# Retention, expert layers and a Mish layer on one core: one PSUM layout for both parts, a product issued earlier, and a table of weight tasks

## Chip, cores and metric

The kernel runs on 1 core of one Trainium2 chip. The metric is the device time of one execution in microseconds (us). A core has engines with instruction queues of their own: PE (matmuls, with weight loads PEld), DVE, ACT, POOL, and SP, which here issues every DMA.

## What is computed

All data is fp32; N = 1152 tokens, model width 512.

```python
# retention: q, k, v of shape (2, 8, 576, 64)
scores = q @ k^T / 8;  ret = scores * gamma_h ** (row - col) for row >= col, else 0
x = (ret @ v), heads side by side, as (1152, 512)
# four experts, w1 (4, 512, 1024), w2 (4, 1024, 512), p = probs / (sum + 1e-9)
x = sum_e p[:, e] * (relu(x @ w1[e]) @ w2[e])
# one layer, w_in (512, 2048), w_out (2048, 512)
out = (h * tanh(softplus(h))) @ w_out,  h = x @ w_in      # Mish
```

## The kernel before, in words

**Order.** The instruction order on every engine is the order of the program text (`manual_schedule`), so each engine works through its list and stands still at an instruction whose inputs are late.

**Retention** (`retention`, until about 57 us): 8 units of two heads. For unit u PE does `scores(u)`, then `values(u-1)` and `cross(u-1)`, then `state(u)`. DVE multiplies the scores by the decay into `ret` (L292, three instructions, here called the eviction of the scores); ACT and DVE read the state into `sbd`; `cross` splits its output into a rounded part (ACT, L191) and the remainder (L192) in `xop` and `xc`. All three kinds of PSUM tile come from one pool `psum` of four two-bank tiles, in rotation. From unit 3 on, each unit also does one weight task, whose remainder goes to DVE.

**Precision.** Each operand is a sum of a rounded part and a remainder, so a product takes three matmuls (L533, L587, L600, L615).

**Feed-forward** (`feed_forward`): 12 units of 512 hidden columns; units 0 to 7 are the experts (NE = 8), 8 to 11 the Mish layer. A list `seq`, made by `steps()`, gives the order of steps:

- `("S", u, c)`, `first_pair`: the first matrix for two thirds of the tokens, as seven products of Strassen's kind (`PRODUCTS`; operands B11, B21, B22 and the differences T1 to T4 in `xop`), 42 matmuls into four banks. Products 1, 5 and 7 are copied out by ACT to p1, p5, p7 (L545); POOL adds p7 and p1 to p5 (L563, L564); DVE adds these to the other banks (L549); then `hidden` makes the activation on ACT (L514, or Mish at L510 and a copy at L511) and its remainder on DVE (L515, L512).
- `("L", u, c)`, `first_last`: the same matrix for the last third, 24 matmuls into a two-bank tile of the pool `pairs` (two such tiles).
- `("Y", u, c, tb)`, `m2`: the second matrix, also into a tile of `pairs`; DVE adds it into `acc` (L662, L663; L671 and L673 in the Mish layer).

After the last expert, `new_x` makes the Mish layer's input from `acc`: differences on DVE (L640), then `split_x`. The steps there run Y(7,0,2), S(8,0), Y(7,1,2), S(8,1), L(8,0), L(8,1). Index i_x is that of Y(7,0,0) in `seq`; S(8,0) is i_x + 5.

**Weight tasks.** A list `tasks` of 96 entries is worked through in order by `weight_task`: either `weight_sums` (four sums on POOL, L134 to L137, which make a "G" matrix out of an "O" matrix) or `split_w` (ACT rounds, L153; POOL makes the remainder in four instructions, L156). A call that finds its task not yet allowed does nothing. Calls stand after steps, and inside `first_pair` in the list `later`, which is emptied behind product 7. The Mish layer's weights come as float64 and are converted by `turn64` (ACT L463 to L466; DVE L451 to L477) through DRAM.

**Pools.** SBUF and PSUM of the retention part are given back at its end; the pools `banks` (four single banks), `pairs`, `hp`, `accp` and `ph` of the feed-forward part take that space.

The functions as the profile numbers their lines:

Of the kernel before, what the change touches and what calls it, by code (L numbers as in the profile page):

```python
# [78 lines left out]
def retention_moe_mish(ctx: ExitStack, tc: tile.TileContext, q2, k2, kt_in, v, vt_in, probs, w1, w2, w64, cdec, dec, out):  # L79
# [86 lines left out]
    def weight_task(i, lo_engine, only_g=False):  # L166
        if n_task[0] >= len(tasks):
            return
        sums, (m, u, c) = tasks[n_task[0]]
        raw = "O" if m == "G" else m, u, c  # L170
        if raw not in raw_t or not (sums or splits((m, u, c), i) and sums_at.get((m, u, c), -99) <= i - (1 if u == 1 else 2)):
# [24 lines left out]

    with ExitStack() as actx:  # L200
        cst = actx.enter_context(tc.tile_pool(name="cst", bufs=1))
        ld = actx.enter_context(tc.tile_pool(name="ld", bufs=2))
        psum = actx.enter_context(tc.tile_pool(name="psum", bufs=4, space=bass.MemoryType.PSUM))

        def ps_tile():
            return psum.tile([P, 2, 512], F32, tag="ps", name="ps")

        units = [(b, pr) for pr in range(NPAIR) for b in range(B)]
# [73 lines left out]
        def scores(u):  # L282
            qr, kb, pr = q_t[u][0], k_t[u % 2], units[u][1]
            a = ps_tile()
            ret = ld.tile([P, 2, 8 * D], F32, tag="ret", name="ret")
            for c, (w, t, off) in enumerate(BLOCKS):
                pe.matmul(  # L287
                    a[:, t, off:off + w], kb[:, c].rearrange("p j d -> p (j d)"),
                    qr[:, c * D:c * D + w], start=True, stop=True,
                )  # L290
            for t, off, n, w, m in EVAC:
                dve.tensor_tensor(  # L292
                    out=ret[:, t, off:off + n * w].rearrange("p (c n) -> p c n", n=w),
                    in0=a[:, t, off:off + n * w].rearrange("p (c n) -> p c n", n=w),
                    in1=cst_sb[:, pr, m:m + w].unsqueeze(1).to_broadcast([P, n, w]), op=ALU.mult,
                )
            ret_t[u] = ret

        def state(u):
            st = ps_tile()  # L300
            vt, kt = q_t[u][1:3]
            sbd, pr = sbd_t[u % 2], units[u][1]
            for c in range(NCH - 1):
                pe.matmul(
                    st[:, 0, c * P:(c + 1) * P], kt[:, c], vt[:, c].rearrange("p j d -> p (j d)"),
                    start=True, stop=True,
                )
            for c in range(NCH - 1):
                for o in own:
                    src = st[o, 0, c * P + o.start:c * P + o.stop]  # L310
# [41 lines left out]
        def retention():  # L352
# [13 lines left out]
            for j in range(2):  # L366
                dve.memset(v_t[1][own[1 - j], :, j], 0.0)


            warm = [ps_tile() for _ in range(4)]  # L370
            for i in range(4):
                pe.matmul(warm[i][:, 0, :256], zero[:, :P], zero, start=True, stop=True)
            prep(0)
# [5 lines left out]
            for u in range(NUN):  # L379
# [11 lines left out]
                if u >= 3:  # L391
                    weight_task(u - NUN - 2, dve)
                if u == 2:
# [11 lines left out]
                if u == 5:  # L405
                    split_x(xop[:, :, T1], t1, dve)
            cross(NUN - 1, values(NUN - 1))
            dve.tensor_tensor(out=t3, in0=t2, in1=t3, op=ALU.subtract)
# [13 lines left out]
    acc_t = acc.rearrange("p k n -> p (k n)").rearrange("p (t d) -> p t d", d=DM)  # L422
    banks = ctx.enter_context(tc.tile_pool(name="banks", bufs=1, space=bass.MemoryType.PSUM))
    pairs = ctx.enter_context(tc.tile_pool(name="pairs", bufs=2, space=bass.MemoryType.PSUM))

    def ps_tile():
        return pairs.tile([P, 2, 512], F32, tag="ps", name="ps")

# [90 lines left out]
    def first_pair(u, c, early, later, order):  # L519


        o = [
            [banks.tile([P, 512], F32, tag=f"b{t}{j}", name=f"b{t}{j}")[:, :TB] for j in range(2)]
            for t in range(2)
        ]
        h = [h_tile(u, c, i) for i in range(2)]

        def product(n):
            m, kh, fb, r, t, j, opens = PRODUCTS[n]
            w = w_t[m, u, c]  # L530
            for kk in range(2):
                for i, (a, b) in enumerate(((0, 1), (0, 0), (1, 0))):
                    pe.matmul(  # L533
                        o[t][j], w[:, a, 2 * kh + kk, fb * P:(fb + 1) * P], xop[:, b, r, kk],
                        start=opens and kk == 0 and i == 0, stop=kk == 1 and i == 2,
                        skip_group_check=not opens,
                    )
            return o[t][j]

        def tile(name):  # L540
            return ph.tile([P, TB], F32, tag=name, name=name, bufs=1)

        def copy(name, src):
            t = tile(name)
            act.activation(out=t, in_=src, func=AF.Copy)  # L545
            return t

        def add(out, a, b):
            dve.tensor_tensor(out=out, in0=a, in1=b, op=ALU.add)  # L549

        done = {}
        for n in order:
            done[n] = product(n)
            if n == 1:
                p1 = copy("p1", done[n])
            elif n == 5:
                p5 = copy("p5", done[n])
                while early:
                    early.pop(0)()
            elif n == 7:  # L560
                p7 = copy("p7", done[n])

                pool.tensor_tensor(out=p5, in0=p5, in1=p7, op=ALU.add)  # L563
                pool.tensor_tensor(out=p5, in0=p5, in1=p1, op=ALU.add)  # L564
                while later:
                    later.pop(0)()
            elif n == 6:
                p16 = tile("p16")
# [37 lines left out]
    def second_t(u, tts):  # L606

        o = ps_tile()
        for n, tt in enumerate(tts):
            ts = slice(tt % 3 * P, (tt % 3 + 1) * P)  # L610
            for f in range(4):
                h, w = h_t[u, f // 2, tt // 3], w_t["W", u, f // 2]
                w = w.rearrange("p a k c -> p a (k c)")
                for i, (a, c) in enumerate(((0, 1), (0, 0), (1, 0))):
                    pe.matmul(  # L615
                        o[:, n], h[:, c, f % 2, ts], w[:, a, f % 2 * 512:(f % 2 + 1) * 512],
                        start=f == 0 and i == 0, stop=f == 3 and i == 2,
                    )
        return o[:, :len(tts)]
# [12 lines left out]
    def new_x(c, tb, a):  # L632
# [10 lines left out]
        if tb == 2:  # L643
            split_x(xc[:, :, 2 * c:2 * c + 2], a, pool)
        elif (c, tb) != (0, 1):
# [31 lines left out]
    def feed_forward():  # L677
# [117 lines left out]
```

## Time and profile before

| | us |
|---|---|
| median of 3 runs (lowest, highest) | 669.52 (666.72, 670.23) |
| profiled execution: its time | 665.34 |
| profiled execution: span, first to last instruction | 663.3 |
| PE busy in the span | 631.9 |
| POOL, DVE, ACT busy in the span | 376.2, 393.0, 309.8 |

The span is what the trace covers; the profiled execution's own time has 2.0 us more around it. Idle time of an engine costs something only where the chain that ends last runs through it.

### The profile page before, as it was taken

The page shows a single profiled execution, that of the slowest core. Times are in us where ns is not written, and L with a number is a line of the kernel's source. Part 1 is how long each engine was busy: PE and PEld are TensorE (multiplying, and loading weights), DVE is VectorE, ACT ScalarE, POOL GpSimd, SP SyncE. Part 2 cuts the span into 40 slices and gives each one's busy share as a digit, 9 for nine tenths or more (in the row PEclk, how much of TensorE's full clock was granted, in tenths as well). Part 3 has the DMA queues.
Part 4 walks back from the last instruction along what each step waited for, and adds up shares of the span by engine and source line. Part 5 has one row for each costly group of instructions (what it writes and reads, how often), then busy time and mean ns, then how long its engine had stood idle before and what let it go on. Part 6 is the DMA issues. An engine that isn't in the chain of part 4 may idle for free.

```text
span 663.3 us, 9398 instructions
## 1 busy us (share of the span) xinstructions
PE 631.9 (95%) x3560; PEld 609.9 (92%) x3560; DVE 393.0 (59%) x593; ACT 309.8 (47%) x503; POOL 376.2 (57%) x471
## 2 busy tenths in 40 slices
PE   8997999999999999999999999968999979998997
PEld 7997999999999999999999999958998768997986
DVE  4776556567665856667776757474356636626322
ACT  4555463625454534635354543225655834745300
POOL 5691877546747638547737728615676465383200
PEclk9999999999999999999999999988999998998999
DMA  8764313243512414422423504200114323130012
GB/s 293 266 239 131 96 62 98 60 132 93 155 61 79 142 51 138 123 92 70 154 65 120 171 0 155 68 0 33 65 32 128 96 95 127 46 113 32 33 48 95
DMA packets 25622, 67.23 MB, mean 101 GB/s; under 512 B 2978, under 2 KB 7146, under 8 KB 25578
## 3 DMA queue, kind: packets, MB, share of 16 engines
q1 hardware_dynamic: 25578, 66.64, 31.1%
q8 instruction: 28, 0.46, 0.3%
q14 instruction: 16, 0.13, 0.1%
HBM read 55.86 MB, written 10.77 MB: 100 GB/s over the span
## 4 chain that ended last, share of the span: by engine, by line
PE 72%; POOL 10%; DVE 6%; issue 5%; ACT 5%; DMA 2%; SPq 1%; POOLq 0%; DVEq 0%
PE ps L600 28%; PE b L533 20%; PE ps L587 13%; PE ps L615 9%; POOL w L156 5%; PE ps L287 1%; ACT w L153 1%; ACT h L511 1%; PE ps L323 1%; ACT b L510 1%; DMA w<-w 1%; POOL wr L135 1%; DVE x L192 1%; DVE b L549 1%; DMA vr<-v 1%
## 5 line engine op out<-in xcount | busy, mean ns | idle before, releaser
L156 POOL TENSOR_TENSOR w<-wr,w 128x256 fp32r<-128x256 f32 x276 | 213.9, 809 | 183.1 <-ACT w L153 183.1
L600 PE MATMUL ps<-h,w 128*128 128x384 f32 x1152 | 203.6, 334 | 0.2 <-DVE h L515 0.2
L600 PEld LDWEIGHTS ps<-h,w 128*128 128x128 f32 x1152 | 200.0, 188 | 0.5 <-DVE h L515 0.5
L533 PE MATMUL b<-x,w 128*128 128x384 f32 x1008 | 181.2, 337 | 11.3 <-ACT p L545 9.0
L533 PEld LDWEIGHTS b<-x,w 128*128 128x128 f32 x1008 | 176.9, 190 | 12.6 <-issue 11.7
L587 PE MATMUL ps<-xc,w 128*128 128x384 f32 x576 | 107.6, 343 | 9.0 <-DVE acc L673 7.4
L587 PEld LDWEIGHTS ps<-xc,w 128*128 128x128 f32 x576 | 103.7, 194 | 10.4 <-DVE acc L673 8.3
L615 PE MATMUL ps<-w,h 128*128 128x512 f32 x432 | 100.2, 390 | 1.3 <-DVE h L512 1.3
L153 ACT ACTIVATE w<-wr 128x1024 fp32r<-128x1024 f32 x72 | 74.4, 1053 | 51.3 <-POOL wr L137 33.8
L615 PEld LDWEIGHTS ps<-w,h 128*128 128x128 f32 x432 | 80.9, 188 | 18.2 <-DVE h L512 1.7
L662 DVE TENSOR_TENSOR ps<-ps,pb 128x768 f32<-128x768 f32 x42 | 40.4, 962 | 34.1 <-PE ps L600 34.1
L545 ACT ACTIVATE p<-b 128x384 f32<-128x384 f32 x72 | 33.7, 490 | 55.8 <-PE b L533 52.5
L515 DVE SCALAR_TENSOR_TENSOR h<-b,h 128x384 fp32r<-128x384 f32 x64 | 34.4, 555 | 39.2 <-ACT h L514 37.8
L514 ACT ACTIVATE h<-b 128x384 fp32r<-128x384 f32 x64 | 30.9, 489 | 41.4 <-DVE b L549 35.6
L549 DVE TENSOR_TENSOR b<-b,p 128x384 f32<-128x384 f32 x72 | 38.8, 559 | 16.4 <-POOL p L564 16.4
L514 ACT ACTIVATE h<-ps 128x768 fp32r<-128x768 f32 x16 | 13.0, 814 | 60.1 <-PE ps L587 60.1
L663 DVE TENSOR_TENSOR acc<-acc,ps 128x768 f32<-128x768 f32 x42 | 40.1, 954 | 1.4
L512 DVE TENSOR_TENSOR h<-b,h 128x384 fp32r<-128x384 f32 x32 | 17.8, 557 | 33.2 <-ACT h L511 33.2
L563 POOL TENSOR_TENSOR p<-p,p 128x384 f32<-128x384 f32 x24 | 24.6, 1024 | 21.7 <-ACT p L545 21.7
L549 DVE TENSOR_TENSOR p<-b,p 128x384 f32<-128x384 f32 x24 | 13.4, 556 | 31.7 <-PE b L533 24.6
L510 ACT ACTIVATE b<-b 128x384 f32<-128x384 f32 x32 | 15.3, 477 | 34.0 <-DVE b L549 28.1
L477 DVE TENSOR_TENSOR g<-g,e 128x512 f32<-128x512 f32 x32 | 30.2, 942 | 1.1
(78 smaller groups left out, 600.4 us busy)
## 6 DMA issues: line engine op xcount, KB each, us to landing
wr<-w SPq DMA_DIRECT2D x32, 512.0 KB, 4.1
w<-w SPq DMA_DIRECT2D x32, 512.0 KB, 4.2
O<-g SPq DMA_DIRECT2D x16, 256.0 KB, 4.3
W<-g SPq DMA_DIRECT2D x16, 256.0 KB, 4.3
wr<-O SPq DMA_DIRECT2D x8, 512.0 KB, 3.3
wr<-W SPq DMA_DIRECT2D x8, 512.0 KB, 3.3
vr<-v SPq DMA_DIRECT2D x8, 288.0 KB, 5.8
pb<-p_dram SPq DMA_DIRECT2D x12, 192.0 KB, 4.8
```

The source lines that it names most:

```text
L153: act.activation(out=w[:, 0], in_=t, func=AF.Copy)
L156: lo_engine.tensor_tensor(out=w[:, 1, k], in0=t[:, k], in1=f32(w[:, 0, k]), op=ALU.subtract)
L514: act.activation(out=out[:, 0], in_=src, func=AF.Relu)
L515: dve.scalar_tensor_tensor(out=out[:, 1], in0=src, scalar=0.0, in1=f32(out[:, 0]), op0=ALU.max, op1=ALU.subtract)
L533: pe.matmul(o[t][j], w[:, a, 2 * kh + kk, fb * P:(fb + 1) * P], xop[:, b, r, kk], start=opens and kk == 0 and i == 0, stop=kk == 1 and i == 2,
L545: act.activation(out=t, in_=src, func=AF.Copy)
L549: dve.tensor_tensor(out=out, in0=a, in1=b, op=ALU.add)
L587: pe.matmul(o[:, j], w[:, a, k, j * P:(j + 1) * P], xc[:, b, k], start=k == 0 and n == 0, stop=k == 3 and n == 2,)
L600: pe.matmul(o[:, j, :TB], w[:, a, 2 * i + f, ds_], h[:, c, f], start=i == f == n == 0, stop=i == f == 1 and n == 2,)
L615: pe.matmul(o[:, n], h[:, c, f % 2, ts], w[:, a, f % 2 * 512:(f % 2 + 1) * 512], start=f == 0 and i == 0, stop=f == 3 and i == 2,)
L662: dve.tensor_tensor(out=o, in0=o, in1=pbb, op=ALU.mult)
L663: dve.tensor_tensor(out=a, in0=a, in1=o, op=ALU.add)
```

## The change

- The pools `banks` and `pairs` are opened ahead of retention and serve both parts. Scores use the two banks `b01` and `b11` (one buffer), the state `b00` and `b10` in turn, values the two tiles of `pairs`.
- Product 1 of S(0,0) and its copy p1 are issued ahead of `values` and `cross` of the last retention unit. p1 and p5 move to a pool `sums` that is open from the start.
- The weight tasks of retention units 6 and 7 put the remainder on POOL.
- In `new_x`, both subtractions for T2 and T4 come one after the other, and the splits of T2, T4 and `xc` are put into `early`, which `first_pair` empties behind product 5's copy.
- `second_t` loops over the halves of the hidden columns outside and the token tiles inside.
- From i_x on, two tables, `n_later` and `n_end`, say how many weight tasks follow product 7 and each step; a split may come one step after its sums.

```diff
-... sums_at.get((m, u, c), -99) <= i - (1 if u == 1 else 2)):
+... sums_at.get((m, u, c), -99) <= i - (1 if u == 1 or u > NE else 2)):
...
+    banks = ... "banks", bufs=1, PSUM;  pairs = ... "pairs", bufs=2, PSUM;  sums = ... "sums", bufs=1
+    def bank(t, j):
+        return banks.tile([P, 512], F32, tag=f"b{t}{j}", name=f"b{t}{j}")
...
-        psum = actx.enter_context(tc.tile_pool(name="psum", bufs=4, ...PSUM))
...
-            a = ps_tile()                      # scores
+            a = [bank(t, 1) for t in range(2)]
...
-            st = ps_tile()                     # state
+            st = bank(u % 2, 0)
...
-                    weight_task(u - NUN - 2, dve)
+                    weight_task(u - NUN - 2, dve if u < 6 else pool)
...
+            o[0][0] = bank(0, 0)[:, :TB]
+            p = product(0, 0, 1, o)
+            ahead_of[0, 0] = o[0][0], p, copy_sum("p1", sums, p)
             cross(NUN - 1, values(NUN - 1))
...
         for n in order:                        # first_pair
-            done[n] = product(n)
+            done[n] = pre[1] if pre and n == 1 else product(u, c, n, o)
             if n == 1:
-                p1 = copy("p1", done[n])
+                p1 = pre[2] if pre else copy_sum("p1", sums, done[n])
...
-        for n, tt in enumerate(tts):           # second_t
-            for f in range(4):
+        for k in range(2):
+            for n, tt in enumerate(tts):
+                for f in range(2):
...
         if tb == 2:                            # new_x
-            split_x(xc[:, :, 2 * c:2 * c + 2], a, pool)
+            early.append(lambda: split_x(xc[:, :, 2 * c:2 * c + 2], a, pool))
...
-            difference(T2, b22, b11)
-            difference(T4, b21, b11)
+            dve.tensor_tensor(out=b11, in0=b22, in1=b11, op=ALU.subtract)
+            dve.tensor_tensor(out=b21, in0=b21, in1=b11, op=ALU.subtract)
+            early.append(lambda: (split_x(xop[:, :, T2], b11, dve), split_x(xop[:, :, T4], b21, dve)))
...
+        n_later = {5: 2, 7: 1, 12: 1, 16: 1, 20: 2, 26: 1, 30: 2, 36: 1}
+        n_end = {0: 1, 8: 2, 10: 2, 14: 2, 17: 1, 18: 1, 21: 1, 23: 2, 27: 1, 28: 1, 31: 1, 33: 1, 34: 1}
...
-                later.extend([lambda: weight_task(i, pool)] * (2 if u in (0, NE) else 1))
+                later.extend([lambda: weight_task(i, pool)] * (n_later.get(i - i_x, 0) if i > i_x else 2 if u == 0 else 1))
...
-            if i_x <= i < i_x + 9:
-                n = (1, 1, 0, 0, 0, 0, 0, 0, 2)[i - i_x]
+            if i >= i_x:
+                n = n_end.get(i - i_x, 0)
...
-                n = 2 if (m, c) == ("L", 0) or u == 0 or u >= NE else 1
+                n = 2 if (m, c) == ("L", 0) or u == 0 else 1
```

## Rows read from the trace of the kernel before

**Rows 1.** Waits of PE, whole span: who waited, for whom; total us, times, longest.

```profile
PE b L533 <- ACT p L545: 9.0, 2, 8.9
PE ps L587 <- DVE acc L673: 7.4, 2, 4.2
PE b L533 <- DVE xc L192: 2.2, 1, 2.2
PE ps L587 <- DVE acc L671: 1.6, 1, 1.6
...
PE ps L615 <- DVE h L512: 1.3, 1, 1.3
```

**Rows 2.** Windows: length; busy us (count) of PE, PEld, DVE, ACT, POOL; granted clock; DMA.

```profile
57.20:59.40 2.20, 0.00 (x1) 0.04 (x1) 1.07 (x3) 1.03 (x3) 0.00 (x0) 1.00 0.41 93
...
86.00:418.00 332.00, 332.00 (x1917) 332.00 (x1917) 222.70 (x311) 155.61 (x241) 208.12 (x256) 1.00 0.33 103
...
441.20:450.00 8.80, 0.01 (x1) 0.00 (x0) 5.58 (x7) 2.98 (x5) 0.37 (x1) 0.64 0.00 0
450.00:452.00 2.00, 1.93 (x6) 1.96 (x7) 0.00 (x0) 1.59 (x2) 1.45 (x1) 0.50 0.00 0
```

**Rows 3.** Chain that ended last: start, us, what; stretches on PE behind its waits.

```profile
547.88 6.74 PE ps L587 x24
...
601.20 5.77 PE ps L587 x24
606.97 8.20 PE ps L615 x36
```

**Rows 4.** Timeline, end of retention: start, us, engine, line, op, count [idle before, releaser].

```profile
46.25 2.22 PE L287 MATMUL ps<-qr,k 128*128 128x128 f32 x18
46.53 1.29 DVE L292 TENSOR_TENSOR ret<-ps,cst_sb 128x384 f32<-128x384 f32 x3
...
51.48 1.23 DVE L156 TENSOR_TENSOR w<-wr,w 128x1024 fp32r<-128x1024 f32 x1 [1.16 <-ACT w L153]
...
53.44 2.29 PE L323 MATMUL ps<-ret,v 128*128 128x128 f32 x18 [1.36 <-DVE ret L292]
...
59.40 2.34 PE L533 MATMUL b<-x,w 128*128 128x384 f32 x12 [2.24 <-DVE xc L192]
...
65.54 0.84 ACT L545 ACTIVATE p<-b 128x384 f32<-128x384 f32 x2
66.06 5.48 PE L533 MATMUL b<-x,w 128*128 128x384 f32 x30 [0.16 <-ACT p L545]
```

**Rows 5.** Timeline between the experts and the Mish layer, step S(8,0).

```profile
441.14 0.94 DVE L640 TENSOR_TENSOR acc<-acc 128x768 f32<-128x768 f32 x1
...
445.85 0.96 DVE L192 TENSOR_TENSOR x<-acc,x 128x768 fp32r<-128x768 f32 x1 [0.91 <-ACT x L191]
...
447.72 0.95 DVE L663 TENSOR_TENSOR acc<-acc,ps 128x768 f32<-128x768 f32 x1
...
449.46 0.85 ACT L545 ACTIVATE p<-b 128x384 f32<-128x384 f32 x2
...
450.07 7.25 PE L533 MATMUL b<-x,w 128*128 128x384 f32 x30 [8.87 <-ACT p L545]
450.33 1.28 ACT L510 ACT_TABLE_LOAD   x1
```

**Rows 6.** Timeline in the Mish layer, steps S(9,1) and S(10,0) and what follows.

```profile
514.23 1.06 ACT L153 ACTIVATE w<-wr 128x1024 fp32r<-128x1024 f32 x1 [3.88 <-POOL wr L137]
...
527.62 8.78 POOL L156 TENSOR_TENSOR w<-wr,w 128x256 fp32r<-128x256 f32 x12 [8.56 <-ACT w L153]
...
539.62 1.01 POOL L563 TENSOR_TENSOR p<-p,p 128x384 f32<-128x384 f32 x1
...
546.61 1.21 DVE L673 TENSOR_TENSOR acc<-acc,ps 128x1024 f32<-128x1024 f32 x1
```

More of the change, by code (lines that the diff above doesn't have):

```diff
@@ L170, in weight_task @@
         raw = "O" if m == "G" else m, u, c
-        if raw not in raw_t or not (sums or splits((m, u, c), i) and sums_at.get((m, u, c), -99) <= i - (1 if u == 1 else 2)):
+        if raw not in raw_t or not (sums or splits((m, u, c), i) and sums_at.get((m, u, c), -99) <= i - (1 if u == 1 or u > NE else 2)):
             return
@@ L194, in retention_moe_mish, with ps_tile, product, sum_tile @@
     ctx.enter_context(tc.manual_schedule())
+    banks = ctx.enter_context(tc.tile_pool(name="banks", bufs=1, space=bass.MemoryType.PSUM))
+    pairs = ctx.enter_context(tc.tile_pool(name="pairs", bufs=2, space=bass.MemoryType.PSUM))
+    sums = ctx.enter_context(tc.tile_pool(name="sums", bufs=1))
+    def bank(t, j):
+        return banks.tile([P, 512], F32, tag=f"b{t}{j}", name=f"b{t}{j}")
+    def ps_tile():
+        return pairs.tile([P, 2, 512], F32, tag="ps", name="ps")
+    def product(u, c, n, o):
+        m, kh, fb, r, t, j, opens = PRODUCTS[n]
+        w = w_t[m, u, c]
+        for kk in range(2):
+            for i, (a, b) in enumerate(((0, 1), (0, 0), (1, 0))):
+                pe.matmul(
+                    o[t][j], w[:, a, 2 * kh + kk, fb * P:(fb + 1) * P], xop[:, b, r, kk],
+                    start=opens and kk == 0 and i == 0, stop=kk == 1 and i == 2,
+                    skip_group_check=not opens,
+                )
+        return o[t][j]
+    def sum_tile(name, of):
+        return of.tile([P, TB], F32, tag=name, name=name, bufs=1)
+    def copy_sum(name, of, src):
+        t = sum_tile(name, of)
+        act.activation(out=t, in_=src, func=AF.Copy)
+        return t
+    ahead_of = {}
     with ExitStack() as actx:
@@ L367, in retention @@
                 dve.memset(v_t[1][own[1 - j], :, j], 0.0)
-            warm = [ps_tile() for _ in range(4)]
             for i in range(4):
-                pe.matmul(warm[i][:, 0, :256], zero[:, :P], zero, start=True, stop=True)
+                pe.matmul(ps_tile()[:, 0, :256], zero[:, :P], zero, start=True, stop=True)
             prep(0)
@@ L406, in retention @@
                     split_x(xop[:, :, T1], t1, dve)
+            o = [[None] * 2 for _ in range(2)]
+            o[0][0] = bank(0, 0)[:, :TB]
+            p = product(0, 0, 1, o)
+            ahead_of[0, 0] = o[0][0], p, copy_sum("p1", sums, p)
             cross(NUN - 1, values(NUN - 1))
@@ L519, in first_pair @@
     def first_pair(u, c, early, later, order):
[L522 to L525, printed above, removed]
+        pre = ahead_of.pop((u, c), None)
+        o = [[pre[0] if pre and t == j == 0 else bank(t, j)[:, :TB] for j in range(2)] for t in range(2)]
         h = [h_tile(u, c, i) for i in range(2)]
[L528 to L546, printed above, removed]
         def add(out, a, b):
@@ L552, in first_pair @@
         for n in order:
-            done[n] = product(n)
+            done[n] = pre[1] if pre and n == 1 else product(u, c, n, o)
             if n == 1:
-                p1 = copy("p1", done[n])
+                p1 = pre[2] if pre else copy_sum("p1", sums, done[n])
             elif n == 5:
-                p5 = copy("p5", done[n])
+                p5 = copy_sum("p5", sums, done[n])
                 while early:
@@ L560, in first_pair @@
             elif n == 7:
-                p7 = copy("p7", done[n])
+                p7 = copy_sum("p7", ph, done[n])
                 pool.tensor_tensor(out=p5, in0=p5, in1=p7, op=ALU.add)
@@ L567, in first_pair @@
             elif n == 6:
-                p16 = tile("p16")
+                p16 = sum_tile("p16", ph)
                 add(p16, done[n], p1)
@@ L608, in second_t @@
         o = ps_tile()
-        for n, tt in enumerate(tts):
-            ts = slice(tt % 3 * P, (tt % 3 + 1) * P)
-            for f in range(4):
[L612 to L618, printed above, removed]
+        for k in range(2):
+            w = w_t["W", u, k].rearrange("p a k c -> p a (k c)")
+            for n, tt in enumerate(tts):
+                h, ts = h_t[u, k, tt // 3], slice(tt % 3 * P, (tt % 3 + 1) * P)
+                for f in range(2):
+                    for i, (a, c) in enumerate(((0, 1), (0, 0), (1, 0))):
+                        pe.matmul(
+                            o[:, n], h[:, c, f, ts], w[:, a, f * 512:(f + 1) * 512],
+                            start=k == f == i == 0, stop=k == f == 1 and i == 2,
+                        )
         return o[:, :len(tts)]
```

15 lines of the change are left out of this document (4 added, 11 removed).

## The prediction

> **What bounds the kernel now.** I read first the windows, to see where PE is full; then the list of PE's waits; then the chain that ended last, for what PE does behind each wait; and last the timeline at each wait, for the reason.
>
> From 86 to 418 us PE is busy without a pause at the full clock: 1917 matmuls in 332 us, 0.173 us each [rows 2]. So a product (6 matmuls) takes 1.04 us, an S step 7.3 us, an L step 4.16 us. In this stretch nothing can be won but by less PE work, and the change removes no matmul. What can be won lies in PE's waits [rows 1], which stand in three places:
>
> - the hand-over from retention to the experts: 2.2 us;
> - S(8,0), the first step of the Mish layer: 8.9 us;
> - the Mish layer: 7.4 us in two waits on L673 (4.2 and so 3.2), 1.6 us on L671 and 1.3 us on L512.
>
> Behind the long ones PE also runs slower. While it stood 8.8 us the granted clock was 0.64 on the mean, and in the next 2 us it was 0.50, the lower level of 1.2 GHz [rows 2]. The 30 matmuls there took 7.25 us; at the full pace they would take 5.2 and the last one's drain of 0.15, so 1.9 us was lost to the clock [rows 5]. The 24 matmuls behind the two L673 waits took 6.74 and 5.77 us in place of 4.16 [rows 3]: 2.6 and 1.6 us lost. All together the waits and the clock hold 21.4 + 6.1 = 27.5 us. That is nearly all that the change can win.
>
> **Part A: retention, PSUM and the early product.** The scores now have one slot, so scores(u+1) cannot start before the eviction of scores(u) has left the first bank. Where is that late? For unit 7: PE issued scores(7) at 46.25, but the eviction of scores(6) began only at 46.53, and its first two of three instructions end near 47.4 [rows 4]. So scores(7) starts about 1.15 us later. Against that, DVE loses the 1.23 us remainder that stood ahead of the eviction of scores(7), and with it the wait of 1.36 us at values(7) [rows 4]. PE's list after 47.4 is scores(7), values(6), cross(6), state(7), some 5.7 us by the starts of before (53.44 less the wait of 1.36, less 46.25, is 5.83), then product 1 (1.04 us): values(7) starts near 54.2 in place of 53.44. cross(7) still ends near 57.15 (59.40 less 2.24), because its last pieces wait for the state's way through ACT and DVE, which the later start does not touch: that chain covers the 0.8 us, and if it did not, they would be paid. The remainder of that weight task on POOL, four pieces of 0.73 us [rows 6], delays the sums queued behind it to about 58 us; those are needed by a split that ACT reaches only at about 63.4 (65.54 less two roundings of 1.06 [rows 4, 6]).
>
> From 57.15 on, product 5 runs at once (its bank is no longer held by the old pool), then the first L step (24 matmuls, issued by `early`) waits for the last `xc` remainder at 59.3, as the products did before. It ends at 63.5, product 2 at 64.5. Product 3 must wait for the copy p5. ACT reaches the p copies at 65.54 behind the splits of T3, T2, T4 and two weight tasks, all unchanged; p5 is now the first of them and ends at 66.0. Before, five products were left at 66.06; now four are left at 66.05. Gain: 1.0 us. Bounds: 0 (the late scores are not covered) to 2.4 us (no wait is left).
>
> **Part B: S(8,0).** Before, ACT's copies p1 and p5 stood at 449.46 behind four splits that each waited on DVE, and product 2 stood behind p1 [rows 5]. Now they stand behind the split of T3 alone, so they are done when products 1 and 5 are (441.2 and 0.5 us more), and products 2, 3 and 7 follow without a wait, to 444.3. DVE: the T2 subtraction starts at 441.14 as before, T4's follows (0.97 each), then the multiply and add of Y(7,0,2) (0.95 each) to 445.0, then the remainders of T2 and T4 (0.96 each) to 446.0 and 446.9. Product 6 waits for T2: 1.7 us. ACT: roundings of T2 and T4 as soon as their subtractions end, then the rounding of `xc`, which needs the add at 445.0, to 445.9; then the table load of 1.28 us, the Mish and its copy, taken at half a microsecond each like a p copy, to 448.2; then p7, to 448.6. Product 4 adds to p7's bank and so waits 1.6 us; it ends at 449.7. Before, the step's 30 matmuls ended at 457.15. Gain: 7.4 us. What is late next is p7, behind the table load. Bounds: 5.5 us (the clock falls again and takes the same 1.9) to 10.8 (8.9 and 1.9: nothing waits). The two waits left are each shorter than the 2.2 us at 57.20, through which the clock stayed at 1.00 [rows 2]; I take 7.4.
>
> The Trainium skill speaks against that: in TensorE: Matmul & The Clock Gate, section HAM oscillation, it says that pauses between bursts of matmuls send the engine back to the slow clock and that this returns pause after pause. By it the sum would be 1.9 us smaller here; the trace has shorter pauses that did not do it and longer ones that did.
>
> **Part C: the Mish layer.** Before, up to two weight tasks followed every step, as early as allowed, so they bunched. At 527.62 twelve remainder pieces ran on POOL for 8.78 us, then four sums to 539.6, and only then L563, the addition to p5 that S(10,0)'s last activations need [rows 6]. The evacuation at 546.61 stands behind these on DVE; PE's next L step wants that tile of `pairs`. Counted through `seq` with both rules, all 96 tasks still get a turn. Behind S(10,0) the tasks of steps i_x+18 and i_x+19 were two W splits, an O split and the sums; now one W split stands there, and the other W and the O split come behind product 7, after POOL's additions. The same holds for S(11,0) ten steps on. So at both places POOL is free when p7 comes, the evacuation moves ahead by some 7 us, more than the wait: 7.4 + 2.6 + 1.6 = 11.6 us.
>
> The 1.6 us at L671 follow from S(9,1), where ACT stood 3.88 us for the sums ahead of a split [rows 6]; those sums now come behind the additions, and the split a step later: 1.55. The 1.3 us on L512 come mostly from the float64 conversions on ACT ahead of the L step's Mish, which stay; only the sums on POOL ahead go. Half: 0.65, with bounds 0 and 1.3. Sum: 13.8 us.
>
> What the later splits cost: W of (9,1) and (10,1) now ends after its Y step begins, some 2.3 us into it. `second_t`'s new order needs it only from half of the first 24 matmuls on, 2.7 us (0.228 each from 36 in 8.20) [rows 3]; I count nothing, with 0.4 us to spare. The split of G(10,0) ends just as product 5 of S(10,0) asks for it. If that cover fails, PE waits up to one split there and in S(11,0): 2 times four pieces of 0.73, 5.8 us, and the clock may fall after each (2.1 on the mean of the two L673 cases): 4.2 more. So the lower bound of C is 3.8, the upper 14.5. SP's queue carries the loads in the same order; each now stands behind a later split, but 4 to 6 steps before its use.
>
> **Sum.** 1.0 + 7.4 + 13.8 = 22.2 us. The profiled execution took 665.34 (span 663.3 and 2.0 around it), so 643.1. The runs' median is 669.52, 4.2 us above it; in the same ratio I forecast 647 us.
>
> **Rivals.**
> 1. *The late splits come too late* (the cover above fails at both places): 22.2 - 10.0 = 12.2 us of gain, 653.1, or 657 on the scale of the median. For it: no margin at G(10,0). Against it: POOL has idle time ahead of each. 0.14.
> 2. *The clock falls in the waits left* in S(8,0) and at the hand-over, 1.9 us each: 18.4 us of gain, 651. For it: two pauses follow each other closely in both places. Against it: the wait at 57.20. 0.12. The page of the Trainium skill named under part B states this rule.
> 3. *PE's waits only move*: the evacuations stay behind the float64 work on DVE and ACT, and the tiles of `pairs` are as late as now; then part C gives about nothing, A and B are lost to new waits for POOL. No change, 669. Against it: the waits follow POOL's additions in the timeline. 0.03.
> 4. *Slower: the table starves the steps.* Each of S(9,1), S(10,0), S(10,1), S(11,0), S(11,1) waits for its G: sums 3.2, rounding 1.06, remainder 2.9 [rows 6], 7.2 us, 36 in all, so 14 us slower, 683. It decides from 4.5 us a place. Against it: the sums come one to three steps (4 to 16 us) ahead of the split, and that again as far ahead of the use. 0.03.
>
> **Chances and range.** The forecast, with part A between its bounds, holds 0.68 (644 to 651). A measurement of this kernel can tell about 0.5% (3.3 us) from no change. Faster: 0.68 + 0.14 + 0.12 = 0.94; same 0.03; slower 0.03. The range goes from 639 (28 us, all waits gone, from the lowest run 666.7) to 657 (rival 1).
>
> **What would show it.** Right: no wait of PE above 2 us behind 60 us; the clock at 1.00 from 441 to the end; POOL's L563 within 1 us of p7 in S(10,0) and S(11,0); scores(7) waiting on L292. In S(8,0) two waits, on T2's remainder (L192) and on p7. Wrong: PE waiting for L156 inside an S or Y step of the Mish layer (rival 1), 0.50 behind S(8,0) (rival 2), or L673 still releasing L587 (rival 3).

## The result and the profile after

The changed kernel takes 649.74 us (median of 4 runs, 647.24 to 652.29) against 669.25 for the kernel before beside it: ratio 0.9714, 95% interval 0.966 to 0.9768. The profiled execution took 647.88 with a span of 645.9, so 17.4 us lie between the two profiles, where the sum said 22.2.

The lines have new numbers in the changed kernel: products L214 (L533 before), L steps L593 (L587), Y steps L606 and L621 (L600, L615), scores L318 and their eviction L323 (L287, L292), p copies L226 (L545), POOL's addition to p5 L569 (L563), Mish remainder L540 (L512), and the evacuation, DVE's add of a Y step into `acc`, L681 (L673). Kernels below shift some of them by a few lines.

First the waits of PE over the whole span of the changed kernel, to be held against [rows 1] (who waited, for whom; total us, times, longest). The wait of 8.9 us on the copies is gone; the two that stand under that name now are one of 2.7 at the hand-over and one of 1.4 in S(8,0). The wait for the evacuation is down from 7.4 to 1.7, but not gone.

```profile
PE b L214 <- ACT p L226: 4.0, 2, 2.7
...
PE b L318 <- DVE ret L323: 2.7, 2, 2.0
...
PE ps L593 <- DVE acc L681: 1.7, 2, 1.3
PE b L214 <- DVE x L192: 1.6, 1, 1.6
...
PE ps L621 <- DVE h L540: 0.6, 1, 0.6
```

Where the 17.4 us come from, by the start of the same step on PE in both traces:

| from, to | before, us | after, us | won | forecast |
|---|---|---|---|---|
| start to S(0,1) | 75.54 | 74.87 | 0.67 | 1.0 (A) |
| S(8,0) to S(8,1) | 22.36 | 17.63 | 4.73 | 7.4 (B) |
| S(9,0) to the last 108 matmuls | 149.48 | 137.63 | 11.85 | 13.8 (C) |

The starts, before and then after (timeline of PE; S(8,0) and S(8,1) of the changed kernel stand under part B; the last group of a window is cut at its end):

```profile
75.54 6.75 PE L533 MATMUL b<-x,w 128*128 128x384 f32 x38
438.96 2.25 PE L533 MATMUL b<-x,w 128*128 128x384 f32 x12
461.32 7.54 PE L533 MATMUL b<-x,w 128*128 128x384 f32 x42
485.22 5.04 PE L533 MATMUL b<-x,w 128*128 128x384 f32 x28
634.70 5.64 PE L615 MATMUL ps<-w,h 128*128 128x512 f32 x24
```

```profile
74.87 7.44 PE L214 MATMUL b<-x,w 128*128 128x384 f32 x42
479.74 7.47 PE L214 MATMUL b<-x,w 128*128 128x384 f32 x42
617.37 22.87 PE L621 MATMUL ps<-w,h 128*128 128x512 f32 x100
```

The three sum to 17.25; the rest is 0.1 us at L(8,0) and the tail. In the profiles each part won, and each won less than forecast.

**Part A in the trace.** The timeline of PE at the end of retention, to be held against [rows 4] (start, us, what, count [idle before, releaser]):

```profile
47.70 2.29 PE L318 MATMUL b<-qr,k 128*128 128x128 f32 x18 [1.99 <-DVE ret L323]
...
57.24 1.34 PE L214 MATMUL b<-x,w 128*128 128x384 f32 x6
58.42 4.32 PE L593 MATMUL ps<-xc,w 128*128 128x384 f32 x24
62.58 1.20 PE L214 MATMUL b<-x,w 128*128 128x384 f32 x6
66.44 4.43 PE L214 MATMUL b<-x,w 128*128 128x384 f32 x24 [2.65 <-ACT p L226]
```

scores(7) waits 1.99 us for the eviction of scores(6). Product 5 follows cross(7) at once, and the first L step starts behind it at 58.42 without the expected wait for the last `xc` remainder; so all the idle time gathers ahead of product 3, 2.65 us where 1.6 was forecast. The order on the engines is the forecast one, the sizes are not. And of the 0.67 us, 0.59 were there at scores(1), the first step that could wait for the one scores slot: it starts at 12.20 here and at 12.79 before, a start that moves from profile to profile (12.20 to 14.21 with the new layout, 12.60 to 13.01 with the old). Counted from scores(1), part A gave 0.08 us.

Why no more? The p copies, on which product 3 waits, stand on ACT behind its read of the last piece of cross(7). The lines are before's read, then the changed kernel's, and the `xc` remainder that the L step was to wait for:

```profile
57.19 0.33 ACT L347 ACTIVATE xf<-ps 128x192 f32<-128x192 f32 x1 [2.00 <-PE ps L333]
```

```profile
57.57 0.33 ACT L378 ACTIVATE xf<-ps 128x192 f32<-128x192 f32 x1 [1.76 <-PE ps L364]
...
59.07 0.56 DVE L192 TENSOR_TENSOR xc<-ps,xc 128x384 fp32r<-128x384 f32 x1 [0.56 <-ACT xc L191]
```

From this read to the products behind the p copies it is 8.87 us in both kernels (66.06 before, 66.44 now). Counted from scores(1), the read comes at 44.40 before and at 45.37 now, 0.97 us later, and that takes back nearly all of the 1.04 us of the product issued early.

**Part B in the trace.** The timeline of PE, to be held against [rows 5], and the windows over the same stretch (columns as in [rows 2]):

```profile
438.31 5.39 PE L214 MATMUL b<-x,w 128*128 128x384 f32 x30
445.28 1.33 PE L214 MATMUL b<-x,w 128*128 128x384 f32 x6 [1.58 <-DVE x L192]
447.98 2.29 PE L214 MATMUL b<-x,w 128*128 128x384 f32 x6 [1.37 <-ACT p L226]
450.06 6.04 PE L606 MATMUL ps<-h,w 128*128 128x384 f32 x24
455.94 7.44 PE L214 MATMUL b<-x,w 128*128 128x384 f32 x42
```

```profile
446.60:448.00 1.40, 0.03 (x2) 0.02 (x1) 0.42 (x1) 1.37 (x4) 1.17 (x1) 0.60 0.04 12
448.00:450.00 2.00, 2.00 (x6) 2.00 (x7) 1.17 (x3) 2.00 (x3) 1.92 (x2) 0.50 0.00 0
```

The one wait of 8.9 us has become the two that were forecast, on T2's remainder (1.58; 1.7 forecast) and on p7 behind the table load (1.37; 1.6 forecast). But the granted clock was 0.60 in the second of them and 0.50 behind it: product 4 took 2.29 us for 1.33, and the 24 matmuls of Y(7,1,2) took 6.04 for 4.32. That is 0.96 + 1.72 = 2.7 us, all that part B lacks.

**Part C in the trace.** PE's first L step of unit 10, which waited 4.2 us before, still waits 1.30 for the evacuation. The chain of work that ended last goes from there back to a load:

```profile
521.49 5.78 DMA wr<-O
...
527.29 1.06 ACT w L153
...
535.79 1.14 DVE acc L681
...
536.97 4.45 PE ps L593 x24
```

The load is that of O(10,1). Its issue waits for a raw tile, which the split of G(10,0) gives back when its remainder ends on POOL; ACT then stands at the rounding of O(10,1), with the Mish work of the same step queued behind it. The timeline shows both ends:

```profile
518.18 6.07 POOL L156 TENSOR_TENSOR w<-wr,w 128x256 fp32r<-128x256 f32 x8 [8.19 <-ACT w L153]
524.20 1.02 POOL L569 TENSOR_TENSOR p<-p,p 128x384 f32<-128x384 f32 x1
...
527.29 1.06 ACT L153 ACTIVATE w<-wr 128x1024 fp32r<-128x1024 f32 x1 [2.51 <-DMA wr<-O]
```

The eight pieces are two remainders; the first, G(10,0)'s, ends near 521.4, and the load starts at 521.49 and lands at 527.27. POOL's additions to p5 (L569) do come early, as forecast. What is late now is a load, and ten steps later once more (0.41).

### The profile page after: what moved, and what is told of

Read it like the earlier page. It is cut to its first block, busy times and chain, and to the rows that moved or that the text cites. A ratio compares the mean times of both kernels' runs of the same rounds, so it can differ in the third digit from the quotient of the medians.

```text
span 645.9 us, 9393 instructions
## 1 busy us (share of the span) xinstructions
PE 628.6 (97%) x3560; PEld 607.1 (94%) x3560; DVE 393.7 (61%) x592; ACT 310.7 (48%) x503; POOL 380.5 (59%) x475
## 4 chain that ended last, share of the span: by engine, by line
PE 74%; POOL 7%; issue 6%; DVE 6%; ACT 4%; DMA 3%; SPq 1%; POOLq 0%; DVEq 0%
PE ps L606 30%; PE b L214 21%; PE ps L593 12%; PE ps L621 8%; POOL w L156 3%; PE ps L354 2%; DMA wr<-O 2%; PE b L318 1%; DVE x L192 1%; ACT h L539 1%; POOL wr L136 1%; PE ps L364 1%; DMA vr<-v 1%; ACT w L153 1%; ACT b L538 1%
## 5 line engine op out<-in xcount | busy, mean ns | idle before, releaser
L156 POOL TENSOR_TENSOR w<-wr,w 128x256 fp32r<-128x256 f32 x280 | 217.9, 814 | 164.8 <-ACT w L153 164.8
L606 PE MATMUL ps<-h,w 128*128 128x384 f32 x1152 | 205.4, 336 | 0.2 <-DVE h L543 0.2
L606 PEld LDWEIGHTS ps<-h,w 128*128 128x128 f32 x1152 | 201.8, 189 | 0.5 <-DVE h L543 0.5
L214 PE MATMUL b<-x,w 128*128 128x384 f32 x1008 | 181.1, 336 | 5.6 <-ACT p L226 4.0
L214 PEld LDWEIGHTS b<-x,w 128*128 128x128 f32 x1008 | 175.9, 189 | 6.9 <-ACT p L226 4.7
L593 PE MATMUL ps<-xc,w 128*128 128x384 f32 x576 | 103.8, 335 | 1.7 <-DVE acc L681 1.7
L593 PEld LDWEIGHTS ps<-xc,w 128*128 128x128 f32 x576 | 100.2, 188 | 2.8 <-DVE acc L681 2.6
L621 PE MATMUL ps<-w,h 128*128 128x512 f32 x432 | 100.3, 390 | 0.6 <-DVE h L540 0.6
L621 PEld LDWEIGHTS ps<-w,h 128*128 128x128 f32 x432 | 80.9, 188 | 17.5 <-DVE h L540 1.0
L226 ACT ACTIVATE p<-b 128x384 f32<-128x384 f32 x72 | 35.2, 491 | 73.5 <-PE b L214 73.1
L540 DVE TENSOR_TENSOR h<-b,h 128x384 fp32r<-128x384 f32 x32 | 17.8, 557 | 32.5 <-ACT h L539 32.4
L569 POOL TENSOR_TENSOR p<-p,p 128x384 f32<-128x384 f32 x24 | 24.6, 1025 | 20.7 <-ACT p L226 20.7
L505 DVE TENSOR_TENSOR g<-g,e 128x512 f32<-128x512 f32 x32 | 30.6, 958 | 1.1
L681 DVE TENSOR_TENSOR acc<-acc,ps 128x1024 f32<-128x1024 f32 (+1 forms) x18 | 17.1, 951 | 22.4 <-PE ps L621 22.4
```

The costliest lines, as they stand in the source:

```text
L156: lo_engine.tensor_tensor(out=w[:, 1, k], in0=t[:, k], in1=f32(w[:, 0, k]), op=ALU.subtract)
L214: pe.matmul(o[t][j], w[:, a, 2 * kh + kk, fb * P:(fb + 1) * P], xop[:, b, r, kk], start=opens and kk == 0 and i == 0, stop=kk == 1 and i == 2,
L593: pe.matmul(o[:, j], w[:, a, k, j * P:(j + 1) * P], xc[:, b, k], start=k == 0 and n == 0, stop=k == 3 and n == 2,)
L606: pe.matmul(o[:, j, :TB], w[:, a, 2 * i + f, ds_], h[:, c, f], start=i == f == n == 0, stop=i == f == 1 and n == 2,)
L621: pe.matmul(o[:, n], h[:, c, f, ts], w[:, a, f * 512:(f + 1) * 512], start=k == f == i == 0, stop=k == f == 1 and i == 2,)
```

## The experiments

Runs are given as median, ratio to the kernel before on the same chip, and 95% interval. Stretches are taken from the profiled execution of each.

**e1_table_only: part C alone.** The kernel before with the new tables and the rule for splits.

```diff
-... sums_at.get((m, u, c), -99) <= i - (1 if u == 1 else 2)):
+... sums_at.get((m, u, c), -99) <= i - (1 if u == 1 or u > NE else 2)):
+        n_later = {5: 2, ...};  n_end = {0: 1, 8: 2, ...}      # as in the change
```

> The kernel before with the new tables of weight tasks alone. By my account the Mish layer holds 12 of the 17.4 us between the two profiled executions and nothing but the table makes them: about 657 us against 669 (ratio 0.982), with both waits of L587 on L673 shrunk to under 1.5 us each and the 8.9 us wait in S(8,0) unchanged. The rival, that the table needs the new loop order of the second matrix to be worth anything, expects new PE waits on L156 at the Y steps behind S(10,0) and S(11,0) of 1 us or more each with the slow clock behind them, and so at most 8 us of gain.

656.42 us, 0.9842 [0.9811, 0.9873]. From S(9,0) to the last 108 matmuls 138.17 us, against 149.48 before and 137.63 with the whole change; PE waits nowhere on a remainder (L156). So part C is the table with its rule for splits; the 0.54 us to the whole change lie in the waits for the O loads (1.30 and 1.00 us here, 1.30 and 0.41 there). S(8,0) is as it was:

```profile
451.26 7.58 PE L533 MATMUL b<-x,w 128*128 128x384 f32 x30 [8.87 <-ACT p L545]
```

**e2_old_second: the change with the old loop order of `second_t`.**

```diff
-        for k in range(2):
-            for n, tt in enumerate(tts):
-                for f in range(2): ...
+        for n, tt in enumerate(tts):
+            for f in range(4): ...
```

> The changed kernel with the old loop order in second_t. My account: the second W split ends about 0.5 us after the old order asks for it in two Y steps, so PE waits 0.5 us twice and loses 1 us, 651 us against 650. The rival that the order matters more expects over 3 us lost; the rival that it does nothing expects no wait of PE on L156 in either step.

650.27 us, 0.9743 [0.9707, 0.978]; 138.22 us from S(9,0) to the last 108 matmuls, with no wait on L156. W(9,1)'s remainder starts on POOL at 527.94 and ends near 530.7, 1.7 us into Y(9,0,0) (528.99): early enough for either order. The two waits of 0.5 us that were expected are not there: the new order does nothing here.

**e3_old_x: the change with `new_x` as before.**

```diff
-            early.append(lambda: split_x(xc[:, :, 2 * c:2 * c + 2], a, pool))
+            split_x(xc[:, :, 2 * c:2 * c + 2], a, pool)
-            dve.tensor_tensor(...);  dve.tensor_tensor(...);  early.append(lambda: (split_x(T2), split_x(T4)))
+            difference(T2, b22, b11);  difference(T4, b21, b11)
```

> The changed kernel with the old order of the splits of T2, T4 and xc. My account: part B is worth 4.7 us net (6.4 of waits less 1.7 for the slower clock in the step behind), all by that order: 654.5 us, one wait of 8 to 9 us in S(8,0) on the p copies. The rival, that the shared PSUM layout or the table gave part of it, expects less than 3 us lost.

657.49 us, 0.9854 [0.9822, 0.9886]. The wait of 8.87 us is back, and S(8,0) to L(8,0) takes 30.6 us where the changed kernel takes 24.9. Part B is the new order of the splits of T2, T4 and `xc`; no run parts the three. The time is 3 us above the expected 654.5: besides S(8,0), the slow clock shows here at the end of retention and at the hand-over (table below).

```profile
453.44 8.10 PE L214 MATMUL b<-x,w 128*128 128x384 f32 x30 [8.87 <-ACT p L226]
```

**e4_no_ahead: the change without the early product 1** (the bank layout stays).

```diff
-            p = product(0, 0, 1, o)
-            ahead_of[0, 0] = o[0][0], p, copy_sum("p1", sums, p)
```

> The changed kernel without product 1 ahead of the last retention unit; the shared PSUM layout stays. My account: the early product is worth one product, 1.0 us, because the step's next four products wait for the copy p5 either way: 651 us, and S(0,1) starts 1.0 us later than in the changed kernel (75.9 for 74.9). The rival, that the shared layout gave the gain and the early product none, expects no difference; a third, that both copies together delay p5, expects 1.5 us.

647.61 us, 0.9715 [0.9681, 0.9749]. From scores(7) to S(0,1) 27.95 us against 27.17 with the early product, so that is worth about 0.8. The 651 us expected did not come, though: by its runs this kernel is as fast as the changed one (ratio 0.9714). What came unasked made up for it. S(8,0) has the same two pauses here as in the changed kernel, and the clock stayed at 1.00 (timeline, then windows):

```profile
446.49 1.33 PE L214 MATMUL b<-x,w 128*128 128x384 f32 x6 [1.58 <-DVE x L192]
449.19 1.31 PE L214 MATMUL b<-x,w 128*128 128x384 f32 x6 [1.37 <-ACT p L226]
450.33 4.32 PE L602 MATMUL ps<-h,w 128*128 128x384 f32 x24
```

```profile
447.80:449.20 1.40, 0.03 (x2) 0.02 (x1) 0.41 (x1) 1.37 (x4) 1.18 (x1) 1.00 0.05 12
...
450.30:452.30 2.00, 2.00 (x14) 2.00 (x13) 1.01 (x3) 1.93 (x4) 1.99 (x3) 1.00 0.00 0
```

S(8,0) to S(8,1) is 14.97 us here, 7.39 less than before: the 7.4 of the forecast.

**e5_split_o_later: O(10,1) and O(11,1) split a step later**, behind Y(9,0,0) and Y(10,0,0) and not behind product 7 of the S step ahead.

```diff
-        n_later = {..., 20: 2, 26: 1, 30: 2, 36: 1};  n_end = {..., 21: 1, ..., 31: 1, ...}
+        n_later = {..., 20: 1, 26: 1, 30: 1, 36: 1};  n_end = {..., 21: 2, ..., 31: 2, ...}
```

> The changed kernel with the O splits of (10,1) and (11,1) one step later than in its table (behind Y(9,0,0) and Y(10,0,0), not behind product 7 of the S steps ahead). My account of the two waits of L593 on L681 (1.3 and 0.4 to 1.0 us): ACT stands 2.5 us at the O split for a DMA that could only be issued when POOL's G split had freed the raw tile, and the Mish work queues behind it; so both PE waits go and the Mish layer, from S(9,0) to the last 108 matmuls, takes 135.9 us in place of 137.6 to 138.2. The rival, that the float64 work on DVE ahead of the evacuation makes these waits, expects them unchanged.

647.12 us, 0.9697 [0.967, 0.9724]. Both waits on the evacuation are gone, and S(9,0) to the last 108 matmuls takes 135.38 us, 14.10 less than before:

```profile
535.10 4.35 PE L593 MATMUL ps<-xc,w 128*128 128x384 f32 x24
...
582.66 4.35 PE L593 MATMUL ps<-xc,w 128*128 128x384 f32 x24
```

**e6_seven_early: product 7 third in S(8,0)**, so that p7 is ahead of the table load.

```diff
-    (1, 5, 2, 3, 7, 6, 4) if late
+    (1, 5, 7, 2, 3, 6, 4) if (u, c) == (NE, 0) else (1, 5, 2, 3, 7, 6, 4) if late
```

> The changed kernel with product 7 ahead of products 2 and 3 in S(8,0), so that p7 is copied ahead of the table load. My account: the second wait of S(8,0), 1.4 us on p7, goes; the first, 1.6 us on the remainder of T2, stays; with one pause in place of two the clock does not fall: S(8,0) and Y(7,1,2) together take 13.2 us (66 matmuls in 11.4 and 1.6 of wait) in place of 17.6, or of 15.0 in the run whose clock held. The rival expects the weight tasks, which now stand ahead of the first Mish on ACT, to make S(8,1) wait for its banks by 1 us or more. If the clock falls all the same, the pair takes 15 us.

648.92 us, 0.9731 [0.9695, 0.9768]. The wait for p7 is gone, the clock holds, and S(8,0) to S(8,1) takes 13.36 us. But the weight tasks behind product 7 now stand ahead of the Mish on ACT, and S(8,1) waits twice for its banks, 0.29 and 1.68 us:

```profile
457.96 5.49 PE L214 MATMUL b<-x,w 128*128 128x384 f32 x30 [1.68 <-DVE h L540]
```

Theory and rival both hold, one after the other: S(8,0) to L(8,0) takes 23.18 us, 1.7 less than in the changed kernel's profile but 0.9 more than in e4, where the clock held with both pauses left in.

**e7_tasks_behind_p5: the two weight tasks ahead of the p copies moved behind p5.**

```diff
-        weight_task(-1, pool);  weight_task(-1, pool);  load_w();  load_w()
-                    early.append(lambda: first_last(0, 0))
+                    early.extend([lambda: weight_task(-1, pool)] * 2 + [load_w] * 2 + [lambda: first_last(0, 0)])
```

> The changed kernel with the two weight tasks at the start of the feed-forward part put behind the copy p5 on ACT. My account: the wait of 2.65 us on the p copies is made of the T splits and these two tasks (2.0 us on ACT); it shrinks to 0.7 us and S(0,1) starts 1.9 us earlier. The rival: the G split, now 0.5 us later, is waited for by product 1 or 5 of S(0,1), or POOL's additions come later by as much as ACT gains, and little is left.

647.81 us, 0.9696 [0.9671, 0.9721]. The wait falls from 2.65 to 0.76, and two new ones ahead of S(0,1)'s banks (0.17 and 0.71), with longer groups around them, give nearly all of it back, as the rival had it: the first Y step starts 24.76 us after product 5, against 24.91 in the changed kernel.

```profile
64.71 4.68 PE L214 MATMUL b<-x,w 128*128 128x384 f32 x24 [0.76 <-ACT p L226]
...
76.82 5.50 PE L214 MATMUL b<-x,w 128*128 128x384 f32 x30 [0.71 <-DVE h L543]
```

**e8_t1_later: the split of T1 a unit later**, away from the eviction that scores(7) waits for.

```diff
-                if u == 5:
+                if u == 6:
```

> The changed kernel with the split of T1 in retention unit 6 in place of 5, so that DVE reaches the eviction of scores(6) 1.5 us earlier. The prediction's account, that the late scores(7) are covered by the chain of the state through ACT and DVE: scores(7) start 1.5 us earlier and nothing behind them does. The rival, that the wait for the one scores slot moves that chain too and is paid in full: everything from scores(7) to S(0,1) starts 1.5 us earlier.

650.09 us, 0.9737 [0.9714, 0.9759]. scores(7) waits 0.51 us in place of 1.4 to 2.3, and yet product 5 starts no earlier: 44.51 us after scores(1), 44.34 in e5. This alone settles little, because T1's split now stands ahead of the next eviction, and cross(7) waits 0.23 us for the state; the table below says more.

**e10_both: the edits of e5 and e6 together**, with the weight tasks of S(8,0) let in behind product 6.

```diff
-                while later:
+                while later and (u, c) != (NE, 0):
                     later.pop(0)()
             elif n == 6:
...
+                while later and (u, c) == (NE, 0):
+                    later.pop(0)()
```

> The changed kernel with the splits of O(10,1) and O(11,1) a step or so later (as in e5_split_o_later) and product 7 of S(8,0) third in its order (as in e6_seven_early), but with the weight tasks of that step let in behind product 6 and not behind product 7. Theory: the weight tasks were what made S(8,1) wait for its banks there, so those waits go. One pause of about 1.3 us is left in S(8,0), the clock stays at 1.00, S(8,0) to L(8,0) takes about 21 us (24.9 in the changed kernel's profile, 22.3 where its clock held, 23.2 in e6), the Mish layer from S(9,0) to the last 108 matmuls 135.4. Span about 640, time 643, 0.963 of the kernel before. Rival: ACT's Mish work is late for S(8,1) whatever stands behind it; S(8,1) waits 1 us or more for a bank as in e6, S(8,0) to L(8,0) stays at 22.5 to 23.2 and the time is about 645.5.

644.6 us, 0.9659 [0.963, 0.9687]. The highest of its six runs (646.1) is below the lowest of the changed kernel (647.24), though on another chip, and the intervals of the two ratios touch. S(8,0) to L(8,0) takes 21.37 us, with the clock at 1.00, and the Mish layer 135.48; S(8,1)'s banks still cost 0.47:

```profile
447.89 2.38 PE L214 MATMUL b<-x,w 128*128 128x384 f32 x12 [1.25 <-DVE x L192]
...
456.98 5.47 PE L214 MATMUL b<-x,w 128*128 128x384 f32 x30 [0.47 <-DVE h L540]
```

The span was 642.8 and not 640: its retention was the slowest but one, as the table below shows.

**e11_old_retention: the change without part A**, that is, the kernel before with the tables and the new order of T2, T4 and `xc` (the diffs of e1 and, reversed, of e3).

> The kernel before with the table of weight tasks and the T2, T4 order, and nothing else of the change: bank layout, order of the last retention unit and hand-over, product 1 and the shift's remainder as before. Theory: part A is worth what its place shows, 0.7 to 1.0 us: the retention part ends as before (product 2 to 8 of S(0,1) at about 75.5 to 76), S(8,0) and the Mish layer as in the changed kernel, time about 650.6, within 0.3% of it. Rival: the bank layout is needed for the gain of the T2, T4 order (a bank that comes free only behind the evictions then stops product 3 to 7 instead of the copy): S(8,0) waits as much as before and the time is 3 us or more above the changed kernel.

649.58 us, 0.9747 [0.9705, 0.9789], 0.16 us from the changed kernel (0.33% by the ratios, within both intervals), though its profile has worse luck with O(10,1), whose load took 6.88 us. S(8,0) has the pauses of 1.58 and 1.37 again, the clock holds, and S(8,0) to S(8,1) takes 14.98 us, 7.38 less than before. So part B does not need the bank layout, and the timeline shows the wait that the late load left:

```profile
448.39 1.31 PE L533 MATMUL b<-x,w 128*128 128x384 f32 x6 [1.37 <-ACT p L545]
449.55 4.32 PE L600 MATMUL ps<-h,w 128*128 128x384 f32 x24
...
535.64 4.46 PE L587 MATMUL ps<-xc,w 128*128 128x384 f32 x24 [2.22 <-DVE acc L674]
```

**e12_both_old_retention: e10 without part A** (e11 with the edits of e5, e6 and e10).

> e10_both without part A: bank layout, order of the last retention unit, hand-over, product 1, the shift's remainders and second_t as in the kernel before; everything else as in e10. Theory (part A is worth nothing, because scores(7) waits 1.4 to 2.2 us for its banks and the one pause of 2.65 us that is left at the hand-over lets the clock fall more often than the old one of 2.24): from scores(1) to products 2 to 8 of S(0,1) 62.7 us, as in the kernel before and in e11 (64.45 in e10, whose clock fell there, 62.0 to 62.7 where it held), the rest as in e10. Span about 641, time 643 to 645, that of e10 within 0.3%. Rival: part A is worth the 1.0 us of the forecast or more, and e10's profile only had a bad one; then this one is 1 us or more slower than e10, 645.6 or above.

644.17 us, 0.9651 [0.9622, 0.9679], span 640.7, the lowest median here, with part A undone, though not clear of e10. S(8,0) to L(8,0) 21.38, S(9,0) to the last 108 matmuls 135.48, as in e10. Its hand-over:

```profile
59.21 2.32 PE L533 MATMUL b<-x,w 128*128 128x384 f32 x12 [2.24 <-DVE xc L192]
...
75.34 6.92 PE L533 MATMUL b<-x,w 128*128 128x384 f32 x39
```

**Part A in all profiles.** Times in us; the third column goes to ACT's read of the last piece of cross(7), the fourth the pause ahead of the products and what the group behind it took.

| kernel | wait of scores(7) | scores(1) to the read of cross(7) | pause, next group | scores(1) to S(0,1) |
|---|---|---|---|---|
| before | none | 44.40 | 2.24, 12 in 2.34 | 62.75 |
| e11, e12 | none | 44.34, 44.22 | 2.24, 12 in 2.32 | 62.68, 62.55 |
| e1 | none | 44.27 | 2.24, 12 in 3.75 | 63.71 |
| changed | 1.99 | 45.37 | 2.65, 24 in 4.43 | 62.67 |
| e5 | 1.36 | 44.67 | 2.65, 24 in 4.45 | 61.99 |
| e2, e6 | 1.38, 1.40 | 44.72, 44.74 | 2.65, 24 in 5.95, 6.00 | 63.54, 63.61 |
| e10 | 2.16 | 45.58 | 2.65, 24 in 6.00 | 64.45 |
| e8 | 0.51 | 44.84 | 2.65, 24 in 6.02 | 63.73 |
| e3 | 2.32, then slow | 47.28 | 2.65, 24 in 6.02 | 66.16 |
| e4 (no early product) | 1.87 | 44.99 | 2.66, 30 in 5.48 | 63.34 |

With the old layout the stretch takes 62.6 to 62.8 us, or 63.7 where the clock fell (once in four). With the new one and the early product it takes 62.0 to 62.7, or 63.5 to 66.2 where it fell (five times in these seven); with the new one alone 63.3 (e4). Left out is e7, which moved the tasks behind the read. In all others but e1, whose clock had fallen, 8.86 or 8.87 us lie between the read and the products behind the p copies, so a later read is paid in full. A wait of scores(7) of 1.4 us moves the read by 0.2 to 0.5 us, one of 2 us by 1.0 to 1.4. The profiles are too few to say how much oftener the clock falls with the new layout.

## Why the prediction was right, point by point

The direction, the order of the parts and the places were right, and 649.74 lies in the range; the likeliest case lay 2.7 us low, and rival 2's 651 was nearer. That the median came so close is partly luck: the profiled execution was forecast at 643.1 and took 647.88, 4.8 us more, but the median lies 1.9 us above it and not the 3.9 that the forecast added.

- **Part A, "Gain: 1.0 us": mis-sized.** It is worth nothing that can be measured: 0.08 us in the profile, and the medians of kernels with and without it differ by 0.16 us (changed and e11) and 0.43 us (e10 and e12, the one without it ahead). Two steps failed. "That chain covers the 0.8 us" named the wrong cover: in the changed kernel cross(7) waits for no state, and PE runs from scores(7) at 47.70 to product 5 at 57.24 without a pause (9.54 to 9.56 us also in e2, e5, e6, e7 and e10), so a late scores(7) is paid behind it. What pays most of it back is the 1.36 us that values(7) no longer waits: nearly enough for a wait of 1.4, not for the 1.99 of this profile. So the p copies were not "all unchanged" but 0.97 us later from scores(1). And "waits for the last `xc` remainder at 59.3" was wrong for the first L step: it starts at 58.42 and never waits for the remainder that ends at 59.63, so the pause that was to be 1.6 us long is 2.65, and the clock fell in it in five of the eight profiles that have it.
- **Part B, 7.4 us: right as a sum, but not in this profile, because the clock fell.** The new order gives 7.38 and 7.39 us where the clock holds (e11, e4), and 4.73 here, below the stated bound of 5.5. That is rival 2 at S(8,0), at 2.65 us and not 1.9. The prediction took the fall for a trait of the kernel, there or not there; the profiles show it in some executions and not in others. The pauses of 1.58 and 1.37 us left the clock at 1.00 in two profiles and pulled it down in five (changed, e2, e5, e7; e8 for a shorter time, 23.82 us from S(8,0) to L(8,0)). Its reason, the 2.2 us at 57.20 "through which the clock stayed at 1.00", does not carry either: in e1 the clock fell behind the same pause.
- **Part C, 13.8 us: right in its mechanism; one step failed.** The table alone gives 11.3 (e1). What lacks is the step "each now stands behind a later split, but 4 to 6 steps before its use": the load of O(10,1) can start only when a raw tile is free, and the later split of G(10,0) gives that tile back too late for a rounding that stands behind product 7. With the rounding moved (e5), part C is 14.10.
- **"`second_t`'s new order needs it only from half ... on": not needed.** The remainder is early enough for the old order (e2).
- **Rivals 1 and 4** did not come: PE waits nowhere on L156. **Rival 3's** sign, the evacuation still releasing an L step, is there with 1.30 and 0.41 us of 7.4; but the cause is the load above and not the float64 work, since both waits go in e5, which leaves that work as it is.
- **What was to be seen:** L569 stands within 1 us of the copy p7, scores(7) waits on the eviction, S(8,0) has the two waits named. Wrong were "no wait of PE above 2 us behind 60 us" (2.65 at 66.44) and "the clock at 1.00 from 441" (0.50 behind S(8,0)).

The lowest mean clock of the changed kernel's runs, 0.988, is in the slowest run, and e12 takes 642.9 us in its two runs at 1.000 and 645.8 in the two at 0.994: part of the spread is how often the clock fell.

## What to carry to other kernels

When splits of weights are spread out, look at what each one gives back: with in-order queues a later split is also a later load, and the rounding that waits for that load holds everything queued behind it on its engine. A long stall that is broken into short ones is not yet safe: where a pause is left, its price is that of the pause and, in some runs, of the slow clock behind it, so count the gain of a shorter pause with that price, or reorder until a pause is gone (e10 and e12 have one pause left in S(8,0), of 1.25 us, and the clock at 1.00 behind it). And a step that starts earlier has a start to be counted from: the 0.67 us of part A were mostly there at scores(1).

## What the hardware showed that was not expected

**The same pauses, two outcomes.** The changed kernel and e4 have the same pauses in S(8,0), to 0.01 us, and the same work on the other engines to 0.01 us in the windows of 1.40 us shown; the clock fell to 0.50 in one and stayed at 1.00 in the other. With the pause of 2.65 us at the hand-over it is alike: the 24 matmuls behind it took 4.43 us in the changed kernel and 5.95 in e2:

```profile
66.54 5.95 PE L214 MATMUL b<-x,w 128*128 128x384 f32 x24 [2.65 <-ACT p L226]
```

One kernel shows both as well: e4's four runs have mean clocks of 1.000, 0.997, 0.992 and 1.000. What decides it stays open. The Trainium skill (TensorE: Matmul & The Clock Gate, section HAM oscillation) tells of a kernel whose longer waits for loads between bursts send the engine back to the slow clock each time; the pauses here are shorter than that kernel's, and at S(8,0) the clock falls behind them in five of seven profiles and holds in two.

**Two engines a few hundredths of a microsecond apart.** Why scores(7) waited 1.99 us in one profile and 1.36 in another with the same text: DVE's remainder of T1 stands ahead of the eviction, and POOL starts a multiplication within 0.07 us of it. The timeline of the changed kernel, and then that of e5:

```profile
45.12 0.73 POOL L298 TENSOR_TENSOR qg<-qr,cst_sb 128x256 f32<-128x256 f32 x1 [0.94 <-PE ps L364]
...
45.19 1.48 DVE L192 TENSOR_TENSOR x<-xf,x 128x768 fp32r<-128x768 f32 x1
```

```profile
45.31 0.94 DVE L192 TENSOR_TENSOR x<-xf,x 128x768 fp32r<-128x768 f32 x1
...
45.33 1.51 POOL L298 TENSOR_TENSOR qg<-qr,cst_sb 128x256 f32<-128x256 f32 x1 [1.02 <-PE ps L364]
```

The one that starts second here takes longer: DVE 1.48 in place of 0.94, or POOL 1.51 in place of 0.73. So it is in e2, e7 and e10 too; in e6 POOL's record starts 0.02 us ahead, and POOL is still the one that takes longer (1.55), so at such a distance the recorded order does not tell. The 0.54 us on DVE are most of the 0.63 by which PE waited longer. The Trainium skill (SBUF — State Buffer, section Who interferes with whom) says that a DVE instruction with two inputs in SBUF contends with a POOL instruction that reads SBUF, over ports that one of them holds alone; the two pairs of rows agree.
